# A clustered attention with feed-forward kernel on one core: the feed-forward epilogue on two tiles at once

## The chip, the cores and the metric

The kernel runs on one core of one Trainium2 chip. The metric is the device time of one execution in microseconds (us); the median of 3 runs counts. A core has five engines with a queue of instructions each: TensorE (PE; its weight loads are shown apart as PEld), VectorE (DVE), ScalarE (ACT), GpSimd (POOL) and SyncE (SP), which here issues all DMAs. Every engine works its queue in order, and an instruction waits for semaphores that other engines raise.

## What is computed

Attention in which a query sees only the keys of its own cluster, for 4 batches of 8 heads with 768 positions of 64, and then a feed-forward layer on the 3072 x 512 result, whose nonlinearity is a ratio of two polynomials.

```python
q_assign = np.argmax(np.einsum('bhsd,hcd->bhsc', q_n, c_n), axis=-1)
k_assign = np.argmax(np.einsum('bhsd,hcd->bhsc', k_n, c_n), axis=-1)
mask = q_assign[:, :, :, None] == k_assign[:, :, None, :]
scores = np.where(mask, scale * np.matmul(q, k.transpose(0, 1, 3, 2)), -1e9)
attn = softmax(scores)
x = np.matmul(attn, v)                 # (3072, 512), heads side by side
h = x @ w_in                           # (3072, 2048)
P = a[0] + a[1] * h + a[2] * h**2 + a[3] * h**3
Q = 1.0 + abs(b[0]) * abs(h) + abs(b[1]) * h**2
out = (P / (Q + 1e-6)) @ w_out
```

`w_in` and `w_out` come as 64-bit floats. The matrices are split into a high and a low f16 part, so that each product of the feed-forward layer is three matmuls (high by high, high by low, low by high).

## The kernel before, in words

**Order.** The whole program is recorded as some 3700 small steps (`op`), each bound to an engine, and written out in the order of the list `ORDER`, which was made ahead of time. There are no loops on the chip. Since each engine runs its own queue in order, the list decides what stands behind what. `K` holds the knobs; `kshare(name, b, i)` gives a knob's share of the steps to one of two engines.

**Stages.** First the weights: 8 blocks (four column blocks of `w_in`, four row blocks of `w_out`), each of four 128x512 tiles. A tile is loaded as 64-bit words (`raw`, 4 KB a partition), its magnitude and sign are taken on ScalarE (L390), its bits are joined on VectorE (L539, L546), the sign is put on by GpSimd (L555), and after a sum of squares on TensorE (L569) the tile is scaled to f16 by ScalarE and its low part made by GpSimd (L606, L613). Batch 0's attention goes beside that (`attend_keys`, with scores and the row maxima at L1278 and L1287). From then on (about 204 us) the feed-forward layer of batch b runs beside the attention of batch b+1 (`attend`: scores on TensorE L1154, maximum on VectorE L1183, exponential on ScalarE, high and low part on ScalarE and VectorE L1214, a transpose by DMA L1221, and the product with v on TensorE L1234). At the end batch 3's feed-forward layer runs alone.

**The feed-forward layer** (`moe`, L1402) takes 256 positions at a time (`tb`, three a batch), and for each of them four blocks of 512 hidden columns (`ci`), each in two halves (`h`). A half is one PSUM bank `ph` of 128x512, made by 24 matmuls (L1441). Out of it ScalarE makes `u` (the absolute value) and `t`, and VectorE multiplies `t` twice (L1458, L1459). The rest, the epilogue, works on memory tiles: a square on GpSimd (two instructions, L1505 and L1506), now and then an added constant on ScalarE (`acq`), Ln and Exp on ScalarE (the reciprocal of Q), an error term (L1523, L1528 on GpSimd, or L1517 on VectorE in the last batch), the product with `u` (L1534, L1535 on GpSimd for the share `mulp`, else L1541 on VectorE), a last product on VectorE (L1546), the f16 high part on ScalarE (L1550) and its low part on GpSimd (L1554; VectorE in the last batch). Then 24 matmuls (L1565) add the half into `po`, which after the fourth block is evicted by ScalarE into `ob` and stored.

**Memory.** `u`, `t` and `s` are three tiles of a ring of 12 slots of 128x512 (2 KB a partition), which the weights use too; in the last batch the second halves take the attention's tiles `sq1`, `sk1`, `sq2`. Raw weights, the loads of v for its largest value (`rvm`) and the results `ob` share two other buffers of 4 KB, `wraw`. The line on which the epilogue's width hangs:

```python
    def wide(name):
        return buf([P, GW, FW], F32, "ring", name, NR)   # GW = kn("gw", 1), FW = 512
```

Of the kernel before, what the change touches and what calls it, by code (L numbers as in the profile page):

```python
# [1654 lines left out]
```

## Time and profile before

| | us |
|---|---|
| median of 3 runs | 938.68 (938.48 to 939.28) |
| the profiled execution | 938.91 |
| its span, first to last instruction | 937.1 |
| TensorE busy | 865.3 (92%) |
| VectorE busy | 840.7 (90%) |
| ScalarE busy | 813.4 (87%) |
| GpSimd busy | 729.5 (78%) |

Busy time is the union of an engine's instructions. A busy share over the span is a mean over stages with different limits, so the rows below take it apart by stretches. A wait is put down to the instruction that came last; idle time of an engine that nobody waits for costs nothing. In a row of the view by line, the names say what is written and read, then come the shape, the count, the busy time in us, the mean in ns of one, and the idle time of the engine just before these instructions.

### The profile page before, as it was taken

How to read it: one execution, taken by the hardware profiler on the slowest of the kernel's cores; microseconds unless marked ns; L12 is line 12 of the kernel's file. 1: busy time of each engine (PE TensorE's matmuls, PEld its weight loads, DVE VectorE, ACT ScalarE, POOL GpSimd, SP SyncE). 2: the span in 40 equal slices, each digit the busy share in tenths (PEclk: the TensorE clock that was granted, in tenths of full speed). 3: DMA queues.
4: the chain of work that ended last, by engine and by line, in shares of the span. 5: the costliest groups of instructions: out<-in, count | busy, mean ns of one | idle time of the engine just before them, and what ended most of it. 6: DMA issues, size and time to landing. Idle time of an engine off the chain costs nothing.

```text
span 937.1 us, 20745 instructions
## 1 busy us (share of the span) xinstructions
PE 865.3 (92%) x7705; PEld 583.9 (62%) x7705; DVE 840.7 (90%) x1503; ACT 813.4 (87%) x1558; POOL 729.5 (78%) x771
## 2 busy tenths in 40 slices
...
GB/s 224 240 205 149 213 138 162 190 206 205 163 121 153 151 155 199 189 145 165 156 153 175 155 158 168 158 176 192 141 154 145 103 154 113 106 29 12 12 24 22
DMA packets 360852, 137.70 MB, mean 147 GB/s; under 512 B 335664, under 2 KB 352048, under 8 KB 360752
## 3 DMA queue, kind: packets, MB, share of 16 engines
...
q8 instruction: 60, 0.98, 0.4%
...
## 4 chain that ended last, share of the span: by engine, by line
PE 51%; DVE 20%; ACT 11%; DMA 8%; issue 5%; POOL 4%; SPq 1%; ACTq 0%; DVEq 0%; POOLq 0%
PE ph L1441 17%; PE po L1565 16%; PE s L1154 6%; PE px L1234 6%; DVE ah L1214 3%; DVE s L1183 3%; DMA rwi<-in_moe_w_in_dram 2%; DVE t L1546 2%; ACT s L390 2%; DVE t L1458 2%; ACT u L390 1%; DVE t L1459 1%; DMA rvm<-in_v_dram 1%; DVE top L1287 1%; ACT ah L390 1%
## 5 line engine op out<-in xcount | busy, mean ns | idle before, releaser
L1441 PE MATMUL ph<-x,win 128*128 128x256 f16 x2304 | 274.0, 274 | 7.7 <-DVE t L1459 5.8
L1441 PEld LDWEIGHTS <-win 128*128 128x128 f16 x2304 | 225.2, 98 | 56.7 <-DVE t L1459 7.5
L1565 PE MATMUL po<-wout,s 128*128 128x512 f16 x1008 | 240.2, 380 | 0.1
L1565 PEld LDWEIGHTS <-s 128*128 128x128 f16 x1008 | 96.9, 98 | 102.4 <-issue 4.5
L1183 DVE TENSOR_SCALAR_CACHE_REDUCE s<-s,cc 128x768 f32<-128x768 f32 x144 | 146.3, 1019 | 15.9 <-PE s L1154 14.7
L1214 DVE SCALAR_TENSOR_TENSOR ah<-s,su,ah 128x768 f16<-128x768 f32 x144 | 144.4, 1010 | 2.8 <-ACT ah L390 2.3
L390 ACT ACTIVATE ah<-s,su 128x768 f16<-128x768 f32 x144 | 128.6, 901 | 8.9 <-DVE su L1202 8.3
L390 ACT ACTIVATE s<-s,nm 128x768 f32<-128x768 f32 x144 | 126.1, 876 | 8.1 <-DVE s L1183 6.2
L1154 PE MATMUL s<-sk,sq 128*128 128x384 f16 x576 | 117.4, 328 | 9.8 <-DVE ah L1214 8.1
L1506 POOL TENSOR_TENSOR s<-s,u 128x512 f32<-128x512 f32 x84 | 113.4, 1350 | 7.0
L1505 POOL TENSOR_SCALAR s<-u,g 128x512 f32<-128x512 f32 x84 | 71.9, 856 | 47.0 <-ACT u L390 32.8
L1528 POOL TENSOR_TENSOR s<-s,u 128x512 f32<-128x512 f32 x72 | 96.7, 1344 | 7.5 <-ACT u L390 7.1
L1554 POOL TENSOR_TENSOR s<-t,s 128x512 f16<-128x512 f32 x72 | 88.2, 1227 | 10.8 <-ACT s L1550 10.7
L1546 DVE SCALAR_TENSOR_TENSOR t<-s,t 128x512 f32<-128x512 f32 x84 | 85.1, 1014 | 0.5 <-POOL s L1528 0.4
L1154 PEld LDWEIGHTS <-sq 128*128 128x128 f16 x576 | 51.9, 98 | 54.0 <-DVE ah L1214 18.4
L1234 PE MATMUL px<-at,vhi 128*64 128x256 f16 x864 | 75.0, 275 | 1.5 <-DVE t L1459 1.0
L1459 DVE SCALAR_TENSOR_TENSOR t<-t,gk,ph 128x512 f32<-128x512 f32 x84 | 62.8, 748 | 3.0
L390 ACT ACTIVATE t<-ph,gk 128x512 f32<-128x512 f32 x84 | 65.4, 780 | 0.0
L390 ACT ACTIVATE u<-ph,gk 128x512 f32<-128x512 f32 x84 | 57.6, 686 | 7.1 <-PE ph L1441 6.5
L1458 DVE SCALAR_TENSOR_TENSOR t<-ph,gk,t 128x512 f32<-128x512 f32 x84 | 62.2, 741 | 1.0 <-ACT t L390 0.7
L1234 PE MATMUL px<-at,vlo 128*64 128x256 f16 x432 | 60.0, 273 | 0.0
L1535 POOL TENSOR_TENSOR t<-t,u 128x512 f32<-128x512 f32 x43 | 56.8, 1321 | 4.0 <-ACT u L390 0.6
...
## 6 DMA issues: line engine op xcount, KB each, us to landing
...
```

The source lines that it names most:

```text
L390: lambda: nc.scalar.activation(out=out(), in_=in_(), func=func, **{a: (x() if callable(x) else x) for a, x in kw.items()}),
L1154: nc.tensor.matmul(sc.ap[:, i, :SH], lhsT=st["q" + x].ap[:, j, t, :], rhs=st["k" + x].ap[:, j, ks, :].rearrange("p t c -> p (t c)"), start ...
L1183: lambda nm=nm, view=view: ts(out=view(), in0=view(), scalar1=cc.ap[:, 0:1], scalar2=None, op0=ALU.mult, op1=ALU.min, accum_out=nm.ap),
L1214: lambda part=part, view=view, su=su: stt(out=part(1), in0=view(), scalar=su.ap, in1=part(0), op0=ALU.mult, op1=ALU.subtract),
L1234: nc.tensor.matmul(px.ap[j * D : (j + 1) * D, :], lhsT=vv.ap[:, j, kt, :], rhs=at[j].ap[:, p_, kt].rearrange("p t c -> p (t c)"), start=(i ...
L1441: nc.tensor.matmul(ph.ap[:, fi * TW : (fi + 1) * TW], lhsT=win[:, wpart, c, f * P : (f + 1) * P], rhs=xs[c].ap[:, xpart], start=(i == 0), ...
L1458: stt(out=t[h].ap, in0=ph.ap, scalar=col("rho")(), in1=t[h].ap, op0=ALU.mult, op1=ALU.mult)
L1506: nc.gpsimd.tensor_tensor(out=sv(), in0=sv(), in1=uv(), op=ALU.mult)
L1528: lambda uv=uv, sv=sv: nc.gpsimd.tensor_tensor(out=sv(), in0=sv(), in1=uv(), op=ALU.mult),
L1546: lambda tv=tv, sv=sv: stt(out=tv(), in0=sv(), scalar=2.0, in1=tv(), op0=ALU.subtract, op1=ALU.mult),
L1554: lambda tv=tv, g16=g16, e=(nc.vector if kshare("gld", b, i_) else nc.gpsimd): e.tensor_tensor(out=g16(1), in0=tv(), in1=g16(0), op=ALU.su ...
L1565: nc.tensor.matmul(po[ti].ap, lhsT=g16(gg)[:, c0 : c0 + P], rhs=wout[:, wpart, f, :], start=(i == 0 and f == 0), stop=(i == 2 and f == NF ...
```

## The change

The epilogue works on two halves at once: `gw` is 2, so `u`, `t` and `s` are 128x1024 tiles (4 KB a partition) and each operation behind the two products on PSUM is one instruction where there were two. The products from PSUM and all matmuls keep their sizes. In the last batch the last block of the last two position groups (`fine`) is still worked in halves, on tiles of the wide size. The weights go through `weights_wide`, which was there and not called: two tiles a step behind the loads.

The ring has nine slots of 4 KB instead of twelve of 2 KB, and with `mw` it takes over what `wraw` held: raw weights, v's loads and the results, the latter two halves in one slot. v's f16 parts have two buffers instead of three (`vn`). In the last batch only block 3 uses the attention's `at` tiles, and every second position group's `po` takes two of the score banks (`swing`).

Shares: the product with `u` is GpSimd's throughout batches 0 to 2 (`mulp` 1 for 0.6); v's scaling is GpSimd's and ScalarE's in one way for all heads (`vsc` 1 for 0.75); the added constant is ScalarE's in half of the pairs instead of three quarters, and in none of batch 0 (`acq`, `acq.0`); half of the last batch's squares are VectorE's (`sqd.3`). The numbers of ns in the steps are entries for the list's planner and do nothing on the chip. `ORDER` is new from end to end.

```diff
-K = {'mulp': 0.6, ... 'vsc': 0.75, ... 'vn': 3, ... 'sqd.3': 0.0, ... 'acq': 0.75, 'T1': 1, 'quick': 1}
+K = {'mulp': 1, ... 'vsc': 1, ... 'vn': 2, ... 'sqd.3': 0.5, ... 'acq': 0.5, 'T1': 1, 'gw': 2, 'mw': 1, 'NR': 9, 'acq.0': 0, 'quick': 1, 'atc': (3,), 'swing': 1, 'fine': 1}
...
+    MERGE = bool(kn("mw"))
+
+    def load(shape, dt, name):
+        return buf(shape, dt, "ring", name, NR) if MERGE else buf(shape, dt, "wraw", name, 2)
...
-                raw = buf([P, 2 * FW], I32, "wraw", "r" + n, 2)
+                raw = load([P, 2 * FW], I32, "r" + n)
...
-        po2 = bank([P, TB, DM], F32, "o", f"po{b}_{tb}", 1)
+        swing = b == B - 1 and tb % 2 and kn("swing")
+        po2 = bank([P, TB, DM], F32, "s" if swing else "o", f"po{b}_{tb}", 2 if swing else 1)
...
-                    if last and GW == 2 and ci % 2:
+                    if last and GW == 2 and ci in kn("atc", (1, 3)):
...
-                if (h + 1) % GW:
+                gw = 1 if last and ci >= NWC - 1 and tb >= NB - kn("fine", 0) else GW
+                if (h + 1) % gw:
                     continue
-                seg = list(u)
-                k = GW - 1
+                seg = list(u) if gw == GW else [h]
+                k = gw - 1
...
-                def view(w_):
-                    return w_.ap.rearrange("p h c -> p (h c)")
+                def view(w_, gw=gw, h=h):
+                    return w_.ap.rearrange("p h c -> p (h c)") if gw == GW else w_.ap[:, h]
...
+        whole = load([P, TB, DM], F32, f"ob{b}_{tb}") if MERGE else None
         for ti in range(TB):
-            ob = buf([P, DM], F32, "wraw", f"ob{b}_{tb}_{ti}", 2)
+            ob = half(whole, ti) if MERGE else load([P, DM], F32, f"ob{b}_{tb}_{ti}")
```

The function that now works the weights, shortened to one pair of tiles:

```python
    def weights_wide(name, i, vt):
...
        ws = [buf([P, GW, FW], I32, "ring", f"w{name}{i}_{q}", NR) for q in range(2)]
        magq = [wide(f"m{name}{i}_{q}") for q in range(2)]
        for q, w in enumerate(ws):
            for h in range(2):
                dma(2000, lambda raw=raw: raw.ap, ...)
                act(668, lambda mags=mags, h=h: mags[h].ap, ..., AF.Copy, ...)
            dve(1050, ... logical_shift_left ...)          # both tiles
            for h, raw in enumerate(raws):
                dve(930, ... logical_shift_right, bitwise_or ...)
                act(668, lambda mags=mags, h=h: mags[h].ap, ..., AF.Sign, ...)
            op("POOL", 2300, ... w * mag ...)              # both tiles
```

How the order moves, at three places. First SP's queue at the start. In the names, `rk0_0` is k of batch 0, head pair 0; `rwi0_1` tile 1 of `w_in`'s block 0; `rwo` the same of `w_out`. Before:

```order
L404 DMA craw_111<-in_centroids_dram 128x64
L404 DMA rk0_0_113<-in_k_dram 128x384 x2
L404 DMA rwi0_0_116<-in_moe_w_in_dram 128x1024
L404 DMA rq0_0_118<-in_q_dram 128x384 x2
L404 DMA rwi0_2_126<-in_moe_w_in_dram 128x1024
L404 DMA ab_96<-in_moe_b_dram 128x2
L404 DMA rwi0_1_168<-in_moe_w_in_dram 128x1024
L404 DMA rk0_1_180<-in_k_dram 128x384
L1018 DMA_TRANSPOSE sk10_0_185<-tk10_0_142 128x12x128
L404 DMA rk0_1_180<-in_k_dram 128x384
L404 DMA rwi0_3_195<-in_moe_w_in_dram 128x1024
```

After:

```order
L386 DMA rk0_0_111<-in_k_dram 128x384
L386 DMA craw_113<-in_centroids_dram 128x64
L386 DMA rq0_0_115<-in_q_dram 128x384
L386 DMA rk0_0_111<-in_k_dram 128x384
L386 DMA rq0_0_115<-in_q_dram 128x384
L386 DMA rwi0_0_119<-in_moe_w_in_dram 128x1024
L386 DMA rwi0_1_121<-in_moe_w_in_dram 128x1024
L386 DMA rwi0_3_126<-in_moe_w_in_dram 128x1024
L386 DMA rwi0_2_131<-in_moe_w_in_dram 128x1024
L1003 DMA_TRANSPOSE sk10_0_183<-tk10_0_145 128x12x128
L386 DMA rk0_1_187<-in_k_dram 128x384 x2
L386 DMA rwo0_1_196<-in_moe_w_out_dram 128x1024
```

The loads of q and k of the first head pair now stand ahead of four weight loads in a row, and the first `w_out` loads follow the first transpose at once.

Second, GpSimd in batch 0's feed-forward layer, around position group 2, block 0; in `s0_2_0_1` the numbers are batch, group, block and half. Before:

```order
L1505 TENSOR_SCALAR s0_2_0_1_4834<-u0_2_0_1_4788,g10_2310 128x512
L1506 TENSOR_TENSOR s0_2_0_1_4834<-s0_2_0_1_4834,u0_2_0_1_4788 128x512
L1554 TENSOR_TENSOR s0_1_3_1_4613<-t0_1_3_1_4580,s0_1_3_1_4613 128x512
L1523 TENSOR_SCALAR s0_2_0_0_4725<-s0_2_0_0_4725,cq_76 128x512
L1534 TENSOR_SCALAR t0_2_0_0_4738<-t0_2_0_0_4738,gk0_2308 128x512
L1535 TENSOR_TENSOR t0_2_0_0_4738<-t0_2_0_0_4738,u0_2_0_0_4718 128x512
L1528 TENSOR_TENSOR s0_2_0_0_4725<-s0_2_0_0_4725,u0_2_0_0_4718 128x512
L1505 TENSOR_SCALAR s0_2_1_0_4954<-u0_2_1_0_4887,g10_2310 128x512
L1506 TENSOR_TENSOR s0_2_1_0_4954<-s0_2_1_0_4954,u0_2_1_0_4887 128x512
L1528 TENSOR_TENSOR s0_2_0_1_4834<-s0_2_0_1_4834,u0_2_0_1_4788 128x512
L1554 TENSOR_TENSOR s0_2_0_0_4725<-t0_2_0_0_4738,s0_2_0_0_4725 128x512
```

After:

```order
L1492 TENSOR_SCALAR s0_2_0_0_4645<-u0_2_0_0_4552,g10_2375 128x1024
L1493 TENSOR_TENSOR s0_2_0_0_4645<-s0_2_0_0_4645,u0_2_0_0_4552 128x1024
L1515 TENSOR_TENSOR s0_1_3_0_4537<-s0_1_3_0_4537,u0_1_3_0_4371 128x1024
L1521 TENSOR_SCALAR t0_1_3_0_4394<-t0_1_3_0_4394,gk0_2373 128x1024
L1522 TENSOR_TENSOR t0_1_3_0_4394<-t0_1_3_0_4394,u0_1_3_0_4371 128x1024
L1510 TENSOR_SCALAR s0_2_0_0_4645<-s0_2_0_0_4645,cq_76 128x1024
L1515 TENSOR_TENSOR s0_2_0_0_4645<-s0_2_0_0_4645,u0_2_0_0_4552 128x1024
L1541 TENSOR_TENSOR s0_1_3_0_4537<-t0_1_3_0_4394,s0_1_3_0_4537 128x1024
L1492 TENSOR_SCALAR s0_2_1_0_4855<-u0_2_1_0_4827,g10_2375 128x1024
L1493 TENSOR_TENSOR s0_2_1_0_4855<-s0_2_1_0_4855,u0_2_1_0_4827 128x1024
L1521 TENSOR_SCALAR t0_2_0_0_4575<-t0_2_0_0_4575,gk0_2373 128x1024
L1522 TENSOR_TENSOR t0_2_0_0_4575<-t0_2_0_0_4575,u0_2_0_0_4552 128x1024
```

Where a half had five to seven instructions of 128x512, a pair has seven of 128x1024; the constant (L1510) and the product with `u` (L1521, L1522) are there for every pair of batch 0.

Third, VectorE's last rows: the last half of batch 3's last group (`3_2_3`), whose tiles before are `sk1` for t and `sq2` for s. Before:

```order
L1458 SCALAR_TENSOR_TENSOR sk13_2_3_13032<-ph3_2_3_1_12984,gk3_8970,sk13_2_3_13032 128x512
L1459 SCALAR_TENSOR_TENSOR sk13_2_3_13032<-sk13_2_3_13032,gk3_8970,ph3_2_3_1_12984 128x512
L1517 SCALAR_TENSOR_TENSOR sq23_2_3_13041<-sq23_2_3_13041,sq13_2_3_13029 128x512
L1541 SCALAR_TENSOR_TENSOR sk13_2_3_13032<-sk13_2_3_13032,gk3_8970,sq13_2_3_13029 128x512
L1546 SCALAR_TENSOR_TENSOR sk13_2_3_13032<-sq23_2_3_13041,sk13_2_3_13032 128x512
L1554 TENSOR_TENSOR sq23_2_3_13041<-sk13_2_3_13032,sq23_2_3_13041 128x512
```

After:

```order
L1444 SCALAR_TENSOR_TENSOR t3_2_3_12221<-ph3_2_3_0_12112,gk3_8873,t3_2_3_12221 128x512
L1445 SCALAR_TENSOR_TENSOR t3_2_3_12221<-t3_2_3_12221,gk3_8873,ph3_2_3_0_12112 128x512
L1479 SCALAR_TENSOR_TENSOR s3_2_3_12202<-u3_2_3_12185,g13_8875 128x512
L1541 TENSOR_TENSOR s3_2_2_0_11797<-t3_2_2_0_11795,s3_2_2_0_11797 128x1024
L1444 SCALAR_TENSOR_TENSOR t3_2_3_12221<-ph3_2_3_1_12128,gk3_8873,t3_2_3_12221 128x512
L1445 SCALAR_TENSOR_TENSOR t3_2_3_12221<-t3_2_3_12221,gk3_8873,ph3_2_3_1_12128 128x512
L1504 SCALAR_TENSOR_TENSOR s3_2_3_12202<-s3_2_3_12202,u3_2_3_12185 128x512
L1528 SCALAR_TENSOR_TENSOR t3_2_3_12221<-t3_2_3_12221,gk3_8873,u3_2_3_12185 128x512 x2
L1533 SCALAR_TENSOR_TENSOR t3_2_3_12221<-s3_2_3_12202,t3_2_3_12221 128x512
L1504 SCALAR_TENSOR_TENSOR s3_2_3_12202<-s3_2_3_12202,u3_2_3_12185 128x512
L1533 SCALAR_TENSOR_TENSOR t3_2_3_12221<-s3_2_3_12202,t3_2_3_12221 128x512
L1541 TENSOR_TENSOR s3_2_3_12202<-t3_2_3_12221,s3_2_3_12202 128x512 x2
```

The last two halves are worked side by side, their squares are VectorE's (L1479), and between them stands the low part of the wide pair `s3_2_2` (L1541).

## Rows read from the trace of the kernel before

**Rows 1.** The page's first part: busy us, share of span, instructions.

```profile
PE 865.3 (92%) x7705; PEld 583.9 (62%) x7705; DVE 840.7 (90%) x1503; ACT 813.4 (87%) x1558; POOL 729.5 (78%) x771
```

**Rows 2.** By stretch: length; busy PE, PEld, DVE, ACT, POOL; clock, DMA share, GB/s.

```profile
0.00:56.00 56.00, 23.47 (x202) 15.02 (x203) 43.30 (x111) 30.01 (x56) 24.87 (x40) 0.96 0.87 224
56.00:204.00 148.00, 135.69 (x1672) 97.71 (x1671) 122.34 (x235) 121.24 (x227) 120.61 (x146) 0.98 0.74 181
204.00:240.00 36.00, 31.64 (x244) 22.25 (x243) 31.66 (x55) 34.25 (x69) 31.56 (x32) 0.95 0.80 176
240.00:800.00 560.00, 544.92 (x4685) 363.42 (x4683) 528.46 (x949) 533.73 (x1051) 496.16 (x509) 1.00 0.85 157
800.00:937.10 137.10, 129.57 (x910) 85.55 (x908) 114.95 (x158) 94.18 (x158) 56.27 (x47) 0.98 0.14 30
```

**Rows 3.** TensorE in order of time at 204 us: start, us, what.

```profile
204.32 1.48 PE L1441 MATMUL ph<-x,win 128*128 128x256 f16 x12
```

**Rows 4.** TensorE's waits, 240 to 800 us: us in total, times, longest.

```profile
PE s L1154 <- DVE ah L1214: 8.1, 14, 1.6
PE ph L1441 <- DVE t L1459: 2.8, 6, 0.7
```

**Rows 5.** ScalarE and VectorE by line, 240 to 800: count, busy us, mean ns, idle.

```profile
L390 ACT ACTIVATE u<-u 128x512 f32<-128x512 f32 x68 | 42.8, 629 | 0.0
...
L390 ACT ACTIVATE s<-s,cq 128x512 f32<-128x512 f32 x51 | 36.9, 724 | 0.4 <-POOL s L1506 0.4
...
L1546 DVE SCALAR_TENSOR_TENSOR t<-s,t 128x512 f32<-128x512 f32 x69 | 71.7, 1041 | 0.4 <-POOL s L1528 0.4
...
L1541 DVE SCALAR_TENSOR_TENSOR t<-t,gk,u 128x512 f32<-128x512 f32 x27 | 34.9, 1294 | 0.3 <-ACT u L390 0.2
```

**Rows 6.** The same view, whole span: prices by size on three engines.

```profile
L1214 DVE SCALAR_TENSOR_TENSOR ah<-s,su,ah 128x768 f16<-128x768 f32 x144 | 144.4, 1010 | 2.8 <-ACT ah L390 2.3
...
L1528 POOL TENSOR_TENSOR s<-s,u 128x512 f32<-128x512 f32 x72 | 96.7, 1344 | 7.5 <-ACT u L390 7.1
L1554 POOL TENSOR_TENSOR s<-t,s 128x512 f16<-128x512 f32 x72 | 88.2, 1227 | 10.8 <-ACT s L1550 10.7
...
L1505 POOL TENSOR_SCALAR s<-u,g 128x512 f32<-128x512 f32 x84 | 71.9, 856 | 47.0 <-ACT u L390 32.8 <-ACT su L390 13.2 <-ACT s L390 0.3
...
L1130 POOL TENSOR_TENSOR vlo<-rv,vhi 128x768 f16<-128x768 f32 x12 | 20.6, 1718 | 0.1
...
L1250 DVE SCALAR_TENSOR_TENSOR x<-px,x 128x256 f16<-128x256 f32 x36 | 14.8, 411 | 0.1
...
L390 ACT ACTIVATE rvm<-rvm 128x768 f32<-128x768 f32 x16 | 13.6, 847 | 4.1 <-DMA rvm<-in_v_dram 4.1
...
L390 ACT ACTIVATE mwi<-rwi 128x512 f32<-128x512 f32 x16 | 10.7, 670 | 10.9 <-DMA rwi<-in_moe_w_in_dram 10.9
...
L1120 POOL TENSOR_SCALAR rv<-rv,ev 128x768 f32<-128x768 f32 x9 | 9.5, 1061 | 0.0
```

**Rows 7.** ScalarE's waits, whole span.

```profile
ACT mwi L390 <- DMA rwi<-in_moe_w_in_dram: 10.9, 9, 2.3
```

**Rows 8.** TensorE's waits, 0 to 56 us.

```profile
PE kt L939 <- ACT tk L390: 10.6, 2, 5.3
```

**Rows 9.** TensorE in order of time, 858 to 933 us; idle before in brackets.

```profile
858.72 0.61 PE L1565 MATMUL po<-wout,sq 128*128 128x512 f16 x2 [1.57 <-ACT sq L1550]
...
930.02 2.75 PE L1565 MATMUL po<-wout,sq 128*128 128x512 f16 x12
```

**Rows 10.** VectorE by line, 800 to 938 us.

```profile
L1541 DVE SCALAR_TENSOR_TENSOR sk<-sk,gk,sq 128x512 f32<-128x512 f32 x12 | 8.9, 745 | 0.2
```

**Rows 11.** Busy time by stretch, 204 to 400 us.

```profile
204.00:400.00 196.00, 186.12 (x1574) 125.70 (x1573) 183.12 (x328) 188.35 (x373) 182.27 (x183) 0.99 0.86 167
```

**Rows 12.** The chain that ended last, 270 to 300 us: start, us, what.

```profile
282.53 2.70 PE po L1565 x12
...
288.87 2.62 PE ph L1441 x24
```

More of the change, by code (lines that the diff above doesn't have):

```diff
@@ L401, in dve, with dma @@
         op("DVE", ns, fn, r, w, vt, claim, chain=chain, n=n)
-    def dma(ns, out, in_, r, w, vt, chain=None):
-        op("SP", ns, lambda: nc.sync.dma_start(out=out(), in_=in_()), r, w, vt, co=w, chain=chain)
+    def dma(ns, out, in_, r, w, vt, chain=None, claim=()):
+        op("SP", ns, lambda: nc.sync.dma_start(out=out(), in_=in_()), r, w, vt, claim=claim, co=w, chain=chain)
     ts, tt, stt = nc.vector.tensor_scalar, nc.vector.tensor_tensor, nc.vector.scalar_tensor_tensor
@@ L647, in weights_wide @@
                     src = moe_w_out[(4 * i + c) * P : (4 * i + c + 1) * P, :]
-                raw = buf([P, 2 * FW], I32, "wraw", "r" + n, 2)
+                raw = load([P, 2 * FW], I32, "r" + n)
                 raws.append(raw)
-                dma(1460, lambda raw=raw: raw.ap, lambda src=src: src.bitcast(I32), [], [raw], vt - kn("wd", 3))
+                dma(2000, lambda raw=raw: raw.ap, lambda src=src: src.bitcast(I32), [], [raw], vt - kn("wd", 3))
                 def high(raw=raw):
@@ L754, in load_v @@
     def load_v(b, hp, why, vt):
-        t = buf([P, 2, NT * D], F32, *(("rv", f"rv{b}_{hp}", kn("rvn", 1)) if why == "u" else ("wraw", f"rvm{b}_{hp}", 2)))
+        if why == "u":
+            t = buf([P, 2, NT * D], F32, "rv", f"rv{b}_{hp}", kn("rvn", 1))
+        else:
+            t = load([P, 2, NT * D], F32, f"rvm{b}_{hp}")
         dma(
-            1100, lambda: t.ap,
+            1500, lambda: t.ap,
             lambda: v[b, 2 * hp : 2 * hp + 2].rearrange("h (p t) d -> p h (t d)", t=NT), [], [t], vt, "v" + why,
@@ L883, in prep @@
                 dma(
[L884 removed]
+                    800,
                     lambda t=raw[nm], j=j: t.ap[:, j],
@@ L1490, in moe @@
                     dve(
-                        (750, 1280)[k] if last else (900, 1600)[k],
+                        (750, 1280)[k] if last else (930, 1780)[k],
                         lambda uv=uv, sv=sv: stt(out=sv(), in0=uv(), scalar=g1c(BT), in1=uv(), op0=ALU.add, op1=ALU.mult),
@@ L1506, in square @@
                         nc.gpsimd.tensor_tensor(out=sv(), in0=sv(), in1=uv(), op=ALU.mult)
-                    op("POOL", (2375, 3600)[k], square, [*us, g1], ss, uu + kb("sq", b), [s_t, u_t])
+                    op("POOL", (2330, 3700)[k], square, [*us, g1], ss, uu + kb("sq", b), [s_t, u_t])
                 acq = kshare("acq", b, i_)
@@ L1515, in moe @@
                     dve(
-                        (840, 1300)[k] if last else (1000, 1800)[k],
+                        (840, 1300)[k] if last else (1000, 1850)[k],
                         lambda uv=uv, sv=sv, acq=acq: stt(out=sv(), in0=sv(), scalar=0.0 if acq else 1.0 + 1e-6, in1=uv(), op0=ALU.add, op1=ALU.mult),
@@ L1544, in moe @@
                 dve(
-                    (840, 1220)[k] if last else (1100, 1700)[k],
+                    (800, 1500)[k] if last else (1080, 2000)[k],
                     lambda tv=tv, sv=sv: stt(out=tv(), in0=sv(), scalar=2.0, in1=tv(), op0=ALU.subtract, op1=ALU.mult),
@@ L1552, in moe @@
                 op(
-                    *(("DVE", (780, 1350)[k]) if kshare("gld", b, i_) else ("POOL", (1231, 2080)[k])),
+                    *(("DVE", (780, 1350)[k]) if kshare("gld", b, i_) else ("POOL", (1231, 2130)[k])),
                     lambda tv=tv, g16=g16, e=(nc.vector if kshare("gld", b, i_) else nc.gpsimd): e.tensor_tensor(
```

21 lines of the change are left out of this document (10 added, 11 removed), and 339 rows, old and new, of the table ORDER.

## Prediction

> **What bounds the kernel now.** I read the page's busy shares first. TensorE is busy 865.3 us of a 937.1 us span, VectorE 840.7, ScalarE 813.4, GpSimd 729.5 [rows 1]. The matmuls are the same in number and shape after the change, so TensorE's busy time is a floor for any order of this program, and what can be won is its idle time: 937.1 - 865.3 = 71.8 us. The stretches of the span say where it lies [rows 2]: 56.0 - 23.5 = 32.5 us before the first softmax rows are ready, 12.3 us up to the first feed-forward matmul at 204 us [rows 3], 4.4 us in the hand-over to 240 us, 15.1 us in the long middle from 240 to 800 us, and 7.5 us from there to the end. The middle is the point of interest: TensorE is busy 97% of it, but ScalarE (533.7 of 560) and VectorE (528.5) are both at 94 to 95%, and GpSimd at 89%. TensorE's waits there are many and short, 8.1 us in 14 waits for VectorE to free a score bank and 2.8 us in 6 waits for VectorE to free a first-layer bank [rows 4]. So TensorE paces the middle, with VectorE and ScalarE just behind it.
>
> **What the change removes, step by step.** First the price of a 128x1024 operation, which no row shows; it lies between twice the 128x512 row and that row plus 512 elements at the slope of nearby sizes.
>
> ScalarE: 128x512 from memory takes 0.629 us, 128x768 0.847 [rows 5, 6], a slope of 0.85 ns an element, so 0.629 + 0.435 = 1.064, and 0.19 us is saved per pair. GpSimd with two tensors and an f16 result: 128x512 and 768 take 1.227 and 1.718 us [rows 6], 1.92 ns an element, so about 2.2 us where two take 2.45; for f32, 1.344 + 512 x 1.92 ns = 2.33, where two take 2.69. GpSimd with one tensor: 0.856 at 512, 1.061 at 768 [rows 6], so some 1.33 for 1.71. Two sizes on one engine show a fixed part each time, which is why I take the slope and not twice the row. VectorE: the last product takes 1.041 us at 512 in the middle [rows 5], and the nearest slope is (1.010 - 0.411)/512 = 1.17 ns an element between the 256 and the 768 row [rows 6]: between 1.64 and 2.08; I take 1.85, about the middle, since no row says which it is nearer to.
>
> ScalarE in the middle: Ln, Exp and cast, some 69 of each, make 34 pairs: 3 x 34 x 0.19 = 20 us. The added-constant pass goes from three in four groups (51 x 0.724 = 36.9 us there [rows 5]) to half the pairs of batches 1 and 2 and none in batch 0: 12 x 1.16 = 14 us. Together 43 us less: 533.7 becomes 491, 88%.
>
> VectorE in the middle: 27 products at 1.294 us go over to GpSimd (34.9 us [rows 5]), and the last product saves 34 x (2.08 - 1.85) = 8 us: 528.5 becomes 486, 87%.
>
> GpSimd takes what the others give up. By the prices above a pair in batches 0 to 2 cost 4.4 (square) + 2.7 (error term) + 0.4 (constant, one group in four) + 0.6 x 4.4 (product) + 2.45 (low half) = 12.6 us. In batch 0, where the constant is now always GpSimd's, it costs 3.66 + 1.33 + 2.33 + 3.66 + 2.2 = 13.2; in batches 1 and 2, 12.5. With 12 pairs a batch that is +7 us in batch 0 and -1 in each of the others; scaling every v tile on GpSimd adds 3 x 1.06. GpSimd's middle rises to about 503 us, 90%.
>
> So where TensorE waited for VectorE it should now wait less. Of the 15.1 us I take off 6, about half of the 10.9 us that those two waits hold; the bounds are 12 (all its named waits gone) and a loss of 8 (the first rival). In order, what is late next is GpSimd.
>
> **The start.** The order of SP's queue puts q's and k's first loads ahead of the weights', and the loads of one weight block no longer wait for two raw buffers, since a ring slot takes them. ScalarE stands 10.9 us waiting for w_in's loads before [rows 7]. But TensorE's longest waits in the first 56 us are for the sums of k on ScalarE (10.6 us in two [rows 8]), a chain that still runs through the same engines, and VectorE now has a 128x1024 shift and four halves ahead of q's low part. I take 0, bounds -4 and +4. Over the whole start GpSimd loses some 16 x (0.36 + 0.38 + 0.25) = 16 us of weight work by the prices above (sign, scale and low part of 16 pairs of tiles) and ScalarE 16 x 0.19 = 3 us; VectorE's own load hardly moves, and from 56 to 204 us it is the busiest helper [rows 2]. I take -3 of 12.3, bounds -8 and +3. For the hand-over I take -1 of 4.4, with -3 and +4: the twelve loads of v for the later batches now stand on SP's queue waiting for ring slots that weight blocks give back, and the transposes of batch 1 are queued behind them.
>
> **The end.** After the last matmul, at 932.8 us, 4.3 us remain for two evictions and two stores, which stay. The rest of the 7.5 us is three waits, the longest 1.57 us [rows 9], each for a low half on VectorE or its cast. The new order puts four second-layer groups, 96 matmuls or 21 us, behind the last first-layer ones, and the last group runs in halves, so its chain (some 9 us) is covered. By the slope above a wide VectorE operation takes 0.745 + 0.6 = 1.35 us here [rows 10]; four of them in 11 groups save 0.14 us each, 6 us, and half of the squares cost 6 x 1.35 = 8 us. I take -2, bounds -3 and +4: the thinnest cover is 14 us of matmuls in front of one group, whose chain (abs 0.7, square 3.7, Ln and Exp 2.2, three products 4.0, cast 1.05) comes to 11.7 us.
>
> **The sum.** 0 - 3 - 1 - 6 - 2 = -12 us on the profiled execution's 938.9 us (span 937.1 and 1.8 around it), 0.2 above the median of the runs: 927 us. The terms' bounds, taken as independent, give 919 to 935 for this case.
>
> **The rivals.** (1) *GpSimd becomes the pace.* From 204 to 400 us it is busy 182.3 of 196 us [rows 11], so idle 13.7. If its idle time cannot shrink, because it comes from handing data back and forth, the 7 us of batch 0 and 1 us of v lengthen that stretch by 8, and the middle loses rather than gains: 938.9 + 8 - 3 - 2 = 942, and up to 950 if the longer chain bites in batches 1 and 2 too. The chain from the last first-layer matmul of a pair to its second layer, abs 0.7, square 3.7, Ln 1.1, Exp 1.1, product and error term 6.0, last product 1.85, cast 1.05, low half 2.2, is 17.7 us against 11 to 12 for one tile; the matmuls that stand between on TensorE's queue, counted in the order and priced by kind [rows 12], are 28 us on average before and 33 us after, so 15 to 17 us are left for queueing in both. It decides if GpSimd cannot be kept busier than 97% of that stretch, 190 of 196 us. Against it: GpSimd stands 10.7 us before casts on ScalarE [rows 6], and ScalarE becomes lighter.
>
> (2) *Larger pieces hold up the engines that have room.* From 0 to 204 us VectorE is at 81% and ScalarE at 74%, and from 800 us at 84% and 69% [rows 2]. There a wide operation saves little, and the wait for its second half is added: a weight pair's shift starts after the second half's pass on ScalarE, 0.67 us later [rows 6], and its sign product after the second sign, another 0.67, so 16 x 1.34 = 21 us spread over two queues, of which I let the start show 6 and the end 3. The middle gains its 6 as before: 938.9 + 9 - 6 = 942 us. The Trainium skill, Perfetto Trace Analysis, section Optimizing Scalar/DVE Operations, says that grouping helps where the engine is saturated, and that breaking instructions up may finish work sooner where ScalarE and VectorE have room but make others wait. By that rule, of which the rows show the first half's condition in the middle and the second half's at both ends, the sum would be this rival's.
>
> (3) *The middle's waits close.* If both helpers at 87 to 88% let TensorE run without gaps, 12 us of the 15.1 go and the start gives its bounds: 938.9 - 12 - 8 - 3 = 916 us.
>
> (4) *The gain goes nowhere.* TensorE's 15.1 us are short waits that a fixed order makes, whatever the load; then only the freed slots move and the time stays at 934 to 941, 938 as its centre.
>
> **How the numbers follow.** The forecast, 927 us, gets 0.50, GpSimd's pace 0.17, larger pieces 0.08, the closed middle 0.14, no effect 0.11. A measurement can tell about 0.2%, 1.9 us, from no change. Faster: 0.50 + 0.14 and 0.04 of rival 4, 0.68. Same: 0.05 of rival 4 and 0.01 of the slower ones, 0.06. Slower: the rest, 0.26. The range reaches down to 914 (half of case 3 and its bound) and up to 946 (most of the first two rivals), leaving out no more than 0.15.
>
> **What would show it.** TensorE's busy time within 3 us of 865. In the middle ScalarE and VectorE at 86 to 89% and GpSimd at 89 to 92%. The waits for VectorE's score bank under 5 us in total. A 128x1024 ScalarE operation at 1.06 us, GpSimd's at 2.2 to 2.35 and 1.33. First feed-forward matmul between 196 and 206 us. The forecast is wrong if GpSimd is 97% busy in batch 0 with TensorE waiting for low halves or for u tiles, if wide operations on GpSimd take twice the narrow ones (batch 0 would then need 186 us for 12 pairs alone), or if TensorE's idle time before 204 us grows.

## The result, and the profile after

The changed kernel is slower: 947.38 us median (946.52 to 948.85) beside 938.58 us for the kernel before on the same chip, a ratio of 1.0096 (95% interval 1.0078 to 1.0113). The forecast was 927 us, with a range up to 946.

The page's first part, after, answers [rows 1]:

```profile
PE 864.7 (92%) x7705; PEld 583.6 (62%) x7705; DVE 826.4 (87%) x1385; ACT 778.7 (82%) x1345; POOL 703.6 (74%) x538
```

TensorE's busy time stayed (864.7 for 865.3) and every other engine became lighter. Yet the span is 944.7 us instead of 937.1. Where TensorE's idle time grew is read from the same stretches as in [rows 2]; the columns are length, then busy us of PE, PEld, DVE, ACT and POOL, clock, DMA share, GB/s:

```profile
0.00:56.00 56.00, 26.17 (x211) 16.64 (x212) 46.86 (x109) 31.38 (x55) 26.18 (x36) 0.95 0.88 231
56.00:204.00 148.00, 133.63 (x1592) 95.15 (x1593) 121.68 (x217) 115.86 (x207) 101.36 (x96) 0.96 0.69 182
204.00:240.00 36.00, 28.32 (x301) 21.75 (x289) 31.81 (x63) 34.03 (x74) 30.56 (x29) 1.00 0.84 176
240.00:800.00 560.00, 537.83 (x4655) 360.17 (x4656) 513.84 (x879) 508.10 (x894) 512.99 (x362) 1.00 0.85 156
800.00:944.80 144.80, 138.79 (x963) 89.90 (x960) 112.17 (x120) 89.36 (x119) 32.48 (x17) 1.00 0.12 28
```

Length less PE's busy time is its idle time. Beside [rows 2] it changed by -2.7 us (0 to 56 us), +2.1 (56 to 204), +3.3 (204 to 240), +7.1 (240 to 800: 22.2 for 15.1) and -1.6 (from 800 to the end at 944.7): +8.2 in all. The middle is most of it, and there ScalarE lost 25.6 us of work, VectorE 14.6, and GpSimd gained 16.8. TensorE's waits in the middle (us in total, times, longest) answer [rows 4]:

```profile
PE s L1139 <- DVE ah L1199: 10.3, 16, 1.2
PE ph L1427 <- DVE x L1235: 4.2, 5, 1.1
PE px L1219 <- DVE t L1445: 2.8, 4, 1.4
PE po L1552 <- POOL s L1541: 2.1, 3, 1.4
```

TensorE waits longer for VectorE, an engine that has less to do. What VectorE spends its time on is told by the view by line of the same stretch, after (count, busy us, mean ns, idle time before):

```profile
L1168 DVE TENSOR_SCALAR_CACHE_REDUCE s<-s,cc 128x768 f32<-128x768 f32 x132 | 133.5, 1019 | 14.0 <-PE s L1139 12.9
L1533 DVE SCALAR_TENSOR_TENSOR t<-s,t 128x1024 f32<-128x1024 f32 x34 | 64.2, 1888 | 1.3 <-POOL t L1522 0.9 <-POOL s L1515 0.3
...
L987 DVE SCALAR_TENSOR_TENSOR tq<-rq,qsc,tq 128x768 f16<-128x768 f32 x10 | 20.9, 2085 | 0.0
...
L987 DVE SCALAR_TENSOR_TENSOR tk<-rk,ksc,tk 128x768 f16<-128x768 f32 x10 | 14.6, 1461 | 0.0
L1059 DVE TENSOR_TENSOR oh<-df,mxi 128x384 f16<-128x384 bf16 x10 | 13.6, 1356 | 0.2
```

Three groups there are not touched by the change in work or shape: the low parts of q and k, and a compare (oh). In the middle of the kernel before they read:

```profile
L1002 DVE SCALAR_TENSOR_TENSOR tq<-rq,qsc,tq 128x768 f16<-128x768 f32 x9 | 11.9, 1327 | 0.0
L1002 DVE SCALAR_TENSOR_TENSOR tk<-rk,ksc,tk 128x768 f16<-128x768 f32 x9 | 11.1, 1234 | 0.0
L1074 DVE TENSOR_TENSOR oh<-df,mxi 128x384 f16<-128x384 bf16 x10 | 7.4, 743 | 0.0
```

These groups take 49.1 us instead of 30.4; count for count (one more tq and one more tk fall into the stretch after) it is 15 us more for the same work. These instructions have one thing in common with the last product (L1533): both inputs lie in the on-chip memory (SBUF). Those that read a PSUM bank keep their price: a softmax row's maximum (L1168) takes 1019 ns, as before. The spread of single instructions shows it best; after the count stand the shortest, median and longest in ns. Kernel before, last product in the ring and in the last batch, and the product with u in both:

```profile
L1546 DVE SCALAR_TENSOR_TENSOR t<-s,t x84: 666/892/1712, 221.9 to 919.9; 128x512 f32<-128x512 f32 x84
...
L1541 DVE SCALAR_TENSOR_TENSOR t<-t,gk,u x41: 739/1099/1977, 219.7 to 918.5; 128x512 f32<-128x512 f32 x41
L1541 DVE SCALAR_TENSOR_TENSOR sk<-sk,gk,sq x12: 732/746/752, 811.5 to 927.2; 128x512 f32<-128x512 f32 x12
```

After, the last product and the maximum on PSUM:

```profile
L1533 DVE SCALAR_TENSOR_TENSOR t<-s,t x49: 691/1226/3415, 235.1 to 932.3; 128x1024 f32<-128x1024 f32 x47, 128x512 f32<-128x512 f32 x2
L1168 DVE TENSOR_SCALAR_CACHE_REDUCE s<-s,cc x144: 995/1020/1028, 188.8 to 817.6; 128x768 f32<-128x768 f32 x144
```

The last product takes 0.67 us (1.21 wide) alone; it ran up to 1.05 us longer before and up to 2.2 us longer after. The product with u ran up to 1.24 us longer before. In order of time, around 333 us after (start, us, engine, what), one sees why:

```profile
332.77 2.35 POOL L1493 TENSOR_TENSOR s<-s,u 128x1024 f32<-128x1024 f32 x1
332.91 3.29 DVE L1533 SCALAR_TENSOR_TENSOR t<-s,t 128x1024 f32<-128x1024 f32 x1
```

GpSimd's instruction began 0.14 us before VectorE's, ran its 2.35 us and ended at 335.12. VectorE's ended 1.08 us after that, at 336.20: it did about all of its 1.2 us of work only when GpSimd was through. At 312 us it went the other way:

```profile
311.92 3.46 POOL L1493 TENSOR_TENSOR s<-s,u 128x1024 f32<-128x1024 f32 x1
311.96 1.21 DVE L1533 SCALAR_TENSOR_TENSOR t<-s,t 128x1024 f32<-128x1024 f32 x1
```

Here VectorE ran in its 1.21 us and GpSimd's took 3.46 where it has 2.35 alone, although its record starts 0.04 us earlier: which of two so close starts goes first cannot be read from the profile's times. The two keep each other out. This agrees with the Trainium skill, SBUF — State Buffer, sections Who interferes with whom and SBUF: two separate sides: a VectorE instruction with two inputs in SBUF contends with a GpSimd instruction that reads SBUF, and the second to issue waits for the whole of the first.

A meeting below is one such VectorE instruction that ran over 0.1 us longer than the shortest of its kind. What meetings cost VectorE in the middle can be worked out from the rows above: count times (mean less the shortest of its kind; 0.99 us for tq and tk, 0.54 and 0.55 for oh). Before, with L1546 and L1541 of [rows 5]: 69 x 0.375 + 27 x 0.555 + 9 x 0.33 + 9 x 0.24 + 10 x 0.20 = 48 us. After: 34 x 0.68 + 10 x 1.09 + 10 x 0.47 + 10 x 0.80 = 47 us. So the sum did not change, though VectorE gave 27 such products away. Taken one by one they are 86 meetings of 0.55 us on average, longest 1.2, before, and 45 of 1.04 us, longest 2.2, after: half as many, each twice as long, as GpSimd's pieces are.

### The profile page after: what moved, and what is told of

Its sections match the earlier page's. It is cut to its first block, busy times and chain, and to the rows that moved or that the text cites. A ratio compares the mean times of both kernels' runs of the same rounds, so it can differ in the third digit from the quotient of the medians.

```text
span 944.7 us, 20112 instructions
## 1 busy us (share of the span) xinstructions
PE 864.7 (92%) x7705; PEld 583.6 (62%) x7705; DVE 826.4 (87%) x1385; ACT 778.7 (82%) x1345; POOL 703.6 (74%) x538
## 4 chain that ended last, share of the span: by engine, by line
PE 42%; DVE 24%; POOL 10%; ACT 10%; issue 9%; DMA 4%; SPq 1%; ACTq 0%; DVEq 0%; POOLq 0%
PE po L1552 14%; PE ph L1427 12%; PE s L1139 5%; PE px L1219 5%; DVE ah L1199 3%; DVE s L1168 3%; ACT s L372 2%; ACT u L372 2%; DVE t L1533 2%; POOL s L1493 2%; DVE t L1444 2%; DVE top L1272 2%; POOL s L1541 1%; DMA sq<-tq 1%; DVE t L1445 1%
## 5 line engine op out<-in xcount | busy, mean ns | idle before, releaser
L1552 PE MATMUL po<-wout,s 128*128 128x512 f16 x1152 | 269.6, 379 | 3.6 <-POOL s L1541 2.1
L1552 PEld LDWEIGHTS <-s 128*128 128x128 f16 x1152 | 111.3, 98 | 121.9 <-POOL s L1541 4.5
L1168 DVE TENSOR_SCALAR_CACHE_REDUCE s<-s,cc 128x768 f32<-128x768 f32 x144 | 145.6, 1019 | 18.6 <-PE s L1139 15.5
L1139 PE MATMUL s<-sk,sq 128*128 128x384 f16 x576 | 117.8, 329 | 14.6 <-DVE ah L1199 12.7
L1492 POOL TENSOR_SCALAR s<-u,g 128x1024 f32<-128x1024 f32 x42 | 55.7, 1327 | 81.8 <-ACT u L372 65.1
L1493 POOL TENSOR_TENSOR s<-s,u 128x1024 f32<-128x1024 f32 x42 | 105.7, 2517 | 3.5
L1515 POOL TENSOR_TENSOR s<-s,u 128x1024 f32<-128x1024 f32 x36 | 87.9, 2443 | 7.8 <-ACT u L372 7.1
L1522 POOL TENSOR_TENSOR t<-t,u 128x1024 f32<-128x1024 f32 x36 | 90.8, 2521 | 3.7 <-ACT u L372 0.8
L1541 POOL TENSOR_TENSOR s<-t,s 128x1024 f16<-128x1024 f32 x36 | 80.2, 2226 | 13.9 <-ACT s L1537 13.8
L1533 DVE SCALAR_TENSOR_TENSOR t<-s,t 128x1024 f32<-128x1024 f32 (+1 forms) x49 | 82.6, 1687 | 1.8 <-POOL t L1522 1.3
L1444 DVE SCALAR_TENSOR_TENSOR t<-ph,gk,t 128x512 f32<-128x512 f32 x96 | 71.1, 741 | 5.0 <-ACT t L372 4.9
L1445 DVE SCALAR_TENSOR_TENSOR t<-t,gk,ph 128x512 f32<-128x512 f32 x96 | 71.8, 748 | 3.4
L1537 ACT CAST s<-t 128x1024 f16<-128x1024 f32 (+1 forms) x49 | 50.2, 1027 | 13.8 <-DVE t L1533 13.8
```

Of the source, the lines that this page charges most:

```text
L1139: nc.tensor.matmul(sc.ap[:, i, :SH], lhsT=st["q" + x].ap[:, j, t, :], rhs=st["k" + x].ap[:, j, ks, :].rearrange("p t c -> p (t c)"), start ...
L1168: lambda nm=nm, view=view: ts(out=view(), in0=view(), scalar1=cc.ap[:, 0:1], scalar2=None, op0=ALU.mult, op1=ALU.min, accum_out=nm.ap),
L1444: stt(out=t[h].ap, in0=ph.ap, scalar=col("rho")(), in1=t[h].ap, op0=ALU.mult, op1=ALU.mult)
L1493: nc.gpsimd.tensor_tensor(out=sv(), in0=sv(), in1=uv(), op=ALU.mult)
L1522: nc.gpsimd.tensor_tensor(out=tv(), in0=tv(), in1=uv(), op=ALU.mult)
L1533: lambda tv=tv, sv=sv: stt(out=tv(), in0=sv(), scalar=2.0, in1=tv(), op0=ALU.subtract, op1=ALU.mult),
```

## Experiments: which engine's load counts

The first theories were that GpSimd's load paces the middle (G), that VectorE's does through the softmax chain (S), that the meetings do (L), and that the order leaves short waits whatever the load (O). Three runs take work from one engine each.

```diff
 # a_poolcut
-                        nc.gpsimd.tensor_scalar(out=tv(), in0=tv(), scalar1=col("a0")(), ...)
 # a_dvecut
-                    stt(out=t[h].ap, in0=t[h].ap, scalar=col("a1")(), in1=ph.ap, ...)
+                    if h == 0:
+                        stt(out=t[h].ap, in0=t[h].ap, scalar=col("a1")(), in1=ph.ap, ...)
 # a_actcut
-                act((630, 1070)[k], uv, uv, AF.Exp, ...)
```

> The changed kernel (947.4 us) without the 36 one-tensor passes of GpSimd in the product with u (L1521, 36 x 1.216 = 44 us of GpSimd's 704; the constant is left out of the product, nothing else). Theory G (GpSimd paces the middle, where it is busy 513 of 560 us): 937 to 941 us. Theory S (VectorE and the softmax chain through it pace it): 945 to 947. Theory L (VectorE and GpSimd keep each other out of memory, and the wide pieces hold longer): 943 to 946. Theory O (the order's own short waits, whatever the load): 946 to 948.

Measured 937.39 us, 10.0 below the changed kernel; ratio to before 0.9984 (0.9969 to 0.9998).

> The changed kernel without VectorE's second product on PSUM for every second half (48 x 0.748 = 36 us of VectorE's 826; that factor of the polynomial is left out there). These instructions have one input in PSUM, none of them ran longer than 0.76 us, so they don't meet GpSimd. G: 945 to 947 us. S: 938 to 941. L: 944 to 946. O: 946 to 948.

Measured 939.75 us, 7.6 below; ratio 1.0012 (0.9998 to 1.0025).

> The changed kernel without the 49 Exp passes of ScalarE in the epilogue (49.4 + 1 us of ScalarE's 779; the reciprocal is left out). It shortens the chain of a pair by 1.05 us too. G: 944 to 947 us. S: 941 to 945, since half the steps of a softmax row are ScalarE's. L: 946 to 947. O: 945 to 948.

Measured 944.60 us, 2.8 below; ratio 1.0052 (1.0033 to 1.0071). That is in G's and in S's range and below L's and O's.

O falls: loads do count. In the first two runs G and S each hit their own number and each miss the other's; L misses both, by 6 and 4 us. GpSimd and VectorE both matter at about the same rate (10.0/44 = 0.23 and 7.6/36 = 0.21 us for one), which neither alone explains, and which two engines that block each other would show.

The fourth run takes the meeting away and leaves the load: an instruction of one input in memory with an accumulated result, at the same price.

```diff
 # a_nolock, batches 0 to 2
-  stt(out=tv(), in0=sv(), scalar=2.0, in1=tv(), op0=ALU.subtract, op1=ALU.mult)
+  ts(out=tv(), in0=sv(), scalar1=2.0, scalar2=None, op0=ALU.subtract, op1=ALU.min, accum_out=accl)
```

> The changed kernel with VectorE's last product of batches 0 to 2 (t<-s,t, two inputs in memory, 36 x 128x1024, 1.2 us alone and up to 3.4 us beside GpSimd) replaced by an instruction of one input with an accumulated result, about 1.1 us and 0.14 us for the accumulator (the product with t is left out). If the two engines' keeping each other out is what costs, its 23 long ones (24 us of excess) and part of GpSimd's 41 us of excess in the middle go. L: 937 to 941 us. G: 942 to 945. S: 941 to 945. O: 946 to 948.

Measured 928.79 us, 18.6 below the changed kernel, about twice the most that L expected; ratio to before 0.9881 (0.9861 to 0.9900). Its last product in the middle, and the accumulator's read:

```profile
L1534 DVE TENSOR_SCALAR_CACHE_REDUCE t<-s 128x1024 f32<-128x1024 f32 x35 | 42.2, 1207 | 0.4 <-POOL t L1523 0.4
...
L1534 DVE DVE_READ_ACCUMULATOR t<-s 128x1 f32 x35 | 2.9, 82 | 0.0
```

The replacement takes 1207 ns, no less than the product alone, and stands at the same place behind the same GpSimd instructions. So no work was saved: what went is the waiting. The middle of this kernel, and TensorE's first waits there:

```profile
240.00:800.00 560.00, 552.97 (x4788) 373.25 (x4785) 494.33 (x929) 519.67 (x914) 497.80 (x369) 1.00 0.86 158
```

```profile
PE s L1140 <- DVE ah L1200: 2.1, 6, 0.5
PE ph L1428 <- DVE x L1236: 1.1, 3, 0.6
```

TensorE's idle time in the middle is 7.0 us instead of 22.2, and its wait for the score bank 2.1 us instead of 10.3.

## Experiments: is it the change, or both kernels?

Both kernels have meetings, so the same edit was made in the kernel before.

> The kernel before with the same replacement as in a_nolock: VectorE's last product of batches 0 to 2 (72 x 128x512) becomes an instruction of one input and an accumulated result (the product with t is left out; 72 x 0.14 = 10 us for the accumulators, twice as many as in a_nolock). Theory L1 (the keeping out costs the changed kernel more, since each piece holds twice as long): 927 to 932 us, a gain of 7 to 11 where a_nolock gained 18.6. Theory L2 (it costs both alike, and something else made the change slower): 918 to 922.

Measured 932.35 us, ratio 0.9926 (0.9907 to 0.9945): a gain of 6.6 us, a little under L1's range, far from L2's. The kernel before still had its 29 products with u (L1541). With these replaced in the same way too:

> b_nolock with VectorE's share of the product with u (29 x 128x512 of batches 0 to 2) also made an instruction of one input (the product is left out), so that neither kernel's epilogue has an instruction of VectorE that meets GpSimd before the last batch. To be held against a_nolock (928.8 us). If the changed kernel's lighter load is worth something once the meetings are gone: 929 to 932, still above it. If all that a_nolock gained on b_nolock came from these 29: 925 to 929.

Measured 929.42 us, ratio 0.9877 (0.9842 to 0.9911), inside the first expectation but by less than the interval can tell. Its middle:

```profile
240.00:800.00 560.00, 550.45 (x4782) 371.48 (x4781) 504.03 (x1058) 540.25 (x1069) 467.04 (x513) 1.00 0.86 159
```

Without the meetings of the epilogue the two kernels take the same time, 0.9881 and 0.9877 of the kernel before; by the two intervals that is known to some 4 us. So the epilogue's meetings cost the kernel before 1 - 0.9877 = 1.2% (11 us) and the changed one 1.0096 - 0.9881 = 2.15% (20 us; 18.6 by the medians). The difference, 9 us, is the whole loss as far as these runs can tell. With no such meetings on either side the lighter loads leave TensorE 2.5 us less idle in the middle of the profiled executions (7.0 for 9.6), and gain nothing that can be told in the whole time. (An accumulator's read is 0.082 us, not the 0.14 expected: 96 of them are 8 us in b_nolock2, 35 are 3 us in a_nolock, about 1 us of time at a_dvecut's rate.)

## Experiments: the length of one hold, or the sum?

```diff
 # a_poolsplit: square, error term, product with u, low half; batches 0 to 2
-  nc.gpsimd.tensor_tensor(out=sv(), in0=sv(), in1=uv(), op=ALU.mult)
+  for j in range(2):
+      c = slice(j * 512, (j + 1) * 512)
+      nc.gpsimd.tensor_tensor(out=sv()[:, c], in0=sv()[:, c], in1=uv()[:, c], op=ALU.mult)
```

> The changed kernel with each wide two-tensor instruction of GpSimd in batches 0 to 2 (4 a pair) issued as two of 128x512 behind each other: no hold longer than 1.27 us instead of 2.36, but some 144 x 0.18 = 25 us more work on GpSimd. Theory L1 (the length of one hold): 941 to 946 us in spite of that work. Theory P (the total time that GpSimd and VectorE's two-input instructions claim; a_poolcut gave 10 us for 44): 951 to 955.

Measured 948.82 us, ratio 1.0105 (1.0086 to 1.0124): between the two, no difference from the changed kernel that can be told. Its middle, VectorE's last product, and ScalarE's longest wait there:

```profile
240.00:800.00 560.00, 536.20 (x4625) 356.52 (x4622) 490.66 (x875) 503.43 (x891) 534.57 (x499) 1.00 0.85 156
```

```profile
L1538 DVE SCALAR_TENSOR_TENSOR t<-s,t 128x1024 f32<-128x1024 f32 x34 | 55.6, 1637 | 10.6 <-POOL s L334 5.8 <-POOL t L334 4.4
```

```profile
ACT u L377 <- POOL s L334: 20.4, 15, 2.6
```

VectorE's product shrank from 1888 to 1637 ns and VectorE's load by 23 us. But GpSimd is now busy 534.6 of 560 us (95%), and ScalarE stands 20.4 us for its squares, which was 4.8 us. One limit took the place of the other. To part them, the split was repeated with the work of a_poolcut away:

> a_poolsplit and a_poolcut together: GpSimd's two-tensor instructions of batches 0 to 2 in halves (no hold over 1.27 us, some 25 us more work) and the 36 one-tensor passes of the product left out (44 us less), so that GpSimd's load, below the changed kernel's, is out of the way. To be held against a_poolcut (937.4 us). Theory L1 (the length of one hold counts): 928 to 934. Theory G or P (only the sum of the work or of the claims counts, 25 us more of it at 0.23): 941 to 945.

Measured 931.17 us (931.13 to 932.05), ratio 0.9912 (0.9889 to 0.9934), 6.2 us below a_poolcut although GpSimd has more to do (508 us in the middle, where a_poolcut has 471). The last product, in a_poolcut and then in a_split_cut:

```profile
L1532 DVE SCALAR_TENSOR_TENSOR t<-s,t 128x1024 f32<-128x1024 f32 x35 | 68.2, 1950 | 0.0
```

```profile
L1537 DVE SCALAR_TENSOR_TENSOR t<-s,t 128x1024 f32<-128x1024 f32 x35 | 55.3, 1579 | 1.5 <-POOL s L334 1.5
```

So shorter pieces pay as long as GpSimd has room for their fixed parts, and GpSimd's work, by which G and P went, is not what decides. That it is the length of one hold alone is not shown: VectorE's waiting, summed as above, fell as well, from 42 us in a_poolcut to 21.

## Experiments: the shares

Two knobs of the change were turned towards their old values or past them, alone and together, in the new order. `mulp` back to 0.6 returns 15 of the 36 products of batches 0 to 2 to VectorE; `acq` at 1 means that the added constant is ScalarE's for every pair, where the kernel before had it so in three quarters.

```diff
 # a_mulp06
-K = {'mulp': 1, ...
+K = {'mulp': 0.6, ...
 # a_acq1: where the constant was GpSimd's (L1510)
+    nc.scalar.activation(out=sv(), in_=sv(), func=AF.Identity, bias=cq)
-    nc.scalar.activation(out=uv(), in_=sv(), func=AF.Ln, bias=cq)
+    nc.scalar.activation(out=uv(), in_=sv(), func=AF.Ln)
-    nc.gpsimd.tensor_scalar(out=sv(), in0=sv(), scalar1=cq, ...)
```

> The changed kernel with the product with u at the share of before (mulp 0.6): some 14 of 36 pairs go back to VectorE, GpSimd loses 14 x 3.6 = 50 us, VectorE gains 14 x 1.3 = 18 us and 14 more instructions that meet GpSimd; the order stays. P: claims fall by 50 - 18 = 32 us at 0.23 us each, against some 4 us for VectorE's load by a_dvecut's rate: 941 to 945 us. G (GpSimd's load alone): 935 to 939. L1 (more meetings): 945 to 950.

Measured 955.60 us, ratio 1.0180 (1.0160 to 1.0200), 8.2 above the changed kernel, beyond even L1. My sum of claims (P) was wrong in sign. Whether it is the meetings or VectorE's load was tried by taking the meetings away:

> a_mulp06 (955.6 us) with both of VectorE's products in the epilogue of batches 0 to 2 made instructions of one input (the other factor is left out in each; 51 x 0.14 us for accumulators). VectorE carries 18 us more than in a_nolock, GpSimd 50 us less. Theory L1 (a_mulp06 was slow through its 15 further meetings): 925 to 933 us. Theory S (through VectorE's load): 938 to 946.

Measured 932.85 us, ratio 0.9932 (0.9905 to 0.9958), 22.7 us below a_mulp06, at the upper edge of L1's range. But this edit takes away all of the epilogue's meetings and not only the 15, so it is to be held against a_nolock: turning `mulp` back costs 8.2 us with the meetings and 4.1 without (7.9 and 4.8 by the ratios). So no more than about half of it hangs on meetings. Nor is there more waiting: VectorE's, summed as above, is 41 us in a_mulp06's middle, where the changed kernel has 47. In the profiled executions 5.8 of the 9.1 us by which a_mulp06's span is longer are TensorE's own busy time (870.5 us for 864.7), at a mean granted clock of 0.984 for 0.991. What makes the rest stays open.

> The same, and the added constant of batches 0 to 2 on ScalarE for every pair (24 x 1.34 = 32 us less GpSimd, 24 x 1.05 = 25 us more ScalarE, which a_actcut priced at 0.06 us each). P: 6 us below a_mulp06, 935 to 939 us. G: 929 to 933. L1: 3 us below a_mulp06, since one-tensor holds are the short ones.

Measured 963.70 us, ratio 1.0265 (1.0245 to 1.0286). It is 8 us above a_mulp06, where all theories expected less. The same move alone:

> The changed kernel (947.4 us) with only the added constant of batches 0 to 2 moved from GpSimd to ScalarE for every pair (24 x 1.34 = 32 us less GpSimd, 24 x 1.05 = 25 us more ScalarE), the product with u all GpSimd's as in the change. By the rates of a_poolcut (0.23 us for one of GpSimd's) and a_actcut (0.06 for one of ScalarE's): 941 to 943 us. If ScalarE's lighter load is what the order needs (a_acq1_mulp06 lost 8 us on a_mulp06 by the same move): 950 to 956.

Measured 957.62 us, ratio 1.0204 (1.0179 to 1.0229), 10.2 above the changed kernel. Its middle, and what VectorE waits for there:

```profile
240.00:800.00 560.00, 528.49 (x4565) 352.59 (x4563) 504.31 (x864) 521.17 (x906) 474.28 (x335) 1.00 0.82 154
```

```profile
DVE su L1187 <- ACT su L372: 18.8, 30, 2.1
DVE ah L1199 <- ACT ah L372: 11.5, 22, 1.5
```

In the changed kernel these two are 12.2 and 5.7 us. Each softmax row goes back and forth between VectorE and ScalarE (maximum, exponential, reciprocal, high part, low part), and ScalarE's added passes stand in that queue. The added pass also makes each pair's own chain longer, which no run took apart from it. Taking ScalarE's work away gains little (a_actcut, 2.8 us for 50), putting work there in this order costs much (10 us for 25), so a rate read from a cut cannot be turned round.

No run with the whole computation in it beat the kernel before.

## Why the prediction was wrong

**The floor and where to look: right.** TensorE's busy time stayed within 1 us, and the middle decided.

**The middle, -6 us: this is the step that failed; +7.1 measured.** It had three parts.

*ScalarE, 533.7 to 491: 508.1 measured.* The prices were right (1.052 us for Exp and 1.046 for the cast, 1.064 estimated). The saving was not: twice a narrow row is not twice its share of the engine, because spans of neighbours overlap. After, in order of time on ScalarE:

```profile
499.22 1.06 ACT L372 ACTIVATE u<-s 128x1024 f32<-128x1024 f32 x1
500.19 0.88 ACT L372 ACTIVATE ah<-s,su 128x768 f16<-128x768 f32 x1
500.97 1.05 ACT L372 ACTIVATE u<-u 128x1024 f32<-128x1024 f32 x1
```

The second starts 0.09 us before the first ends, the third 0.10 before the second. So a pair saves some 0.19 - 0.09 = 0.10 us an operation, 34 x 3 x 0.10 = 10 us instead of 20. The constant's passes fell by the forecast 23 us, from 36.9 to 13.7, but 39 fewer of them are 39 fewer overlaps, some 4 us. That makes 29, and 25.6 was measured; the rest was not taken apart.

*VectorE, 528.5 to 486: 513.8 measured.* The 34.9 us of products went, and the last product's price was near (1.89 for 1.85), but by chance: alone it takes 1.21 us, and the rest is waiting for GpSimd. What the step left out is that those meetings move to other instructions and get longer: tq, tk and oh took 18.7 us more (15 count for count). The rows on record had the sign of it. The same product was 1.294 us in the middle [rows 5] and 0.745 in the last batch [rows 10], where GpSimd is mostly idle. I took both as prices and did not ask why they differ. What is left of the gap is overlap again: added up one by one, VectorE's instructions in the middle take 593.7 us before and 570.5 after, 23 us less, where its busy time fell by 14.6.

*GpSimd, 503: 513.0 measured.* Alone its wide operations are 2.35, 2.13 and 1.12 us (2.33, 2.2 and 1.33 estimated); the two-tensor f32 ones average 2.45 to 2.54, again the meetings.

From these loads I concluded that TensorE would wait less for VectorE. It waited 10.3 us for the score bank instead of under 5, since a late VectorE is late by up to 2.2 us at a time. a_nolock leaves 7.0 us of TensorE's idle time in the middle, below the 9.1 forecast, but the 15.1 us of before hold meetings too. Against b_nolock2's 9.6 us the lighter loads bring 2.5 us. So the step failed twice: it left out that wider pieces keep VectorE out longer, and it took 6 us for what is worth 2.5 without that.

**The start, 0 and -3: -2.7 and +2.1 measured.** Together -0.6, no gain. In the kernels derived from the changed one these two stretches have 29.5 to 31.4 and 13.1 to 15.4 us of idle time, in those from the kernel before 30.6 to 32.5 and 12.3 to 12.9, so a part of each difference is only the execution. GpSimd's 19 us less in the second stretch bought nothing: VectorE, with 121.7 us as before, is the busiest helper there, as the prediction itself said. The first feed-forward matmul came at 204.7 us (204.3 before).

**The hand-over, -1: +3.3 measured,** near its bound of +4. All kernels of the changed order have 6.2 to 7.7 us of idle time there, those of the old one 4.4 to 4.6. This is the order's, and no run was made on which of its steps it is; it stays open.

**The end, -2: -1.6 measured.** The cover that the prediction counted held: after 918.38 us TensorE runs 102 second-layer matmuls without a stop.

**The sum's own slips.** The terms' bounds, added in squares as independent ones, run from 918 to about 945 us and not from 919 to 935. By its two rows GpSimd's one-tensor operation comes to 0.856 + 512 x 0.80 ns = 1.27 us and not 1.33. Neither decides: 947.4 lies above both ranges, and 0.06 us an operation is small beside the terms that failed.

**The rivals.** (1) named the right sign and range (942 to 950) and the right engine, but not the mechanism: from 204 to 400 us GpSimd is busy 182.6 of 196 us, as in [rows 11], below the 190 from which it was to decide, and the loss is spread (+2.3, +3.4 and +2.3 us of TensorE's idle time from 240, 400 and 560 us, 160 us each). (2) named larger pieces, but by another mechanism, the wait for a pair's second half, and in another place: the start and the end stood still, and the middle, to which it gave its 6 us, lost as GpSimd's larger pieces kept VectorE out for longer. The Trainium skill, Perfetto Trace Analysis, section Optimizing Scalar/DVE Operations, says that grouping can improve throughput where the engine is saturated. Here, with VectorE and ScalarE at 94 to 95% of the middle, ScalarE's busy time there did fall by 25.6 us, and yet the kernel's time rose. The same section says that moving work between VectorE and GpSimd may not help since they share a read port. No run here shows that move by itself in the old order; in the new one a_mulp06, which takes 15 products back, was slower too. (3) did not come about even without the epilogue's meetings: a_nolock took 928.8 us for its 916 and left 7.0 us idle in the middle for its 3. (4) is right on the loads alone: a_nolock and b_nolock2 can't be told apart.
